# Regrouped PSUM banks, a new TensorE order and earlier loads in a fused attention and mixer kernel

## The chip, the cores and the metric

The kernel runs on one core of a Trainium2 chip. The metric is the device time of one execution in microseconds (us). The kernel before takes 413.0 us (median of three runs, 410.32 to 413.69). Executions are called fast unless the record says otherwise. A profiled execution gives a span a little shorter than its time (414.7 us span for 416.4 us of time).

## The reference

Random-feature attention for 8 batches of 8 heads, 576 positions, head size 64, 128 features; its output x, 8 x 576 x 512, goes through a low-rank mixer and a feed-forward layer of width 2048.

```python
def phi(x):
    proj = np.einsum('bhsd,md->bhsm', x, omega)
    return np.concatenate([np.cos(proj), np.sin(proj)], axis=-1) / np.sqrt(m)
q_p, k_p = phi(q), phi(k)
kv  = np.einsum('bhsm,bhsd->bhmd', k_p, v);  z = np.sum(k_p, axis=2)
num = np.einsum('bhsm,bhmd->bhsd', q_p, kv); den = np.einsum('bhsm,bhm->bhs', q_p, z)
x   = num / den                                  # then (batch, seq, 512)
h   = x.transpose(0, 2, 1) @ U @ V               # rank 32, mixes positions
u   = x + h.transpose(0, 2, 1)
out = u + np.maximum(u @ w_ch1, 0.0) @ w_ch2     # 512 -> 2048 -> 512
```

## The kernel before

The work is cut into 32 groups g (a batch and two heads) and into 43 blocks s, issued in a fixed order on each engine. Block s of the steady part does the angles, sines and cosines of group s, `key_values` and `numerators` of group s - 1, two pairs of hidden tiles (W1) of an earlier batch, and one W2 sum of 16 matmuls in three parts. Every fourth block also mixes a batch (`mix_in`, three `mix_out`). q, k, v come in quads (loads that hold four heads), so quad n serves groups 2n and 2n + 1: GpSimd issues the load that casts them to bf16, and SyncE issues the DMA transposes of k and q. (The first and the fourth quad are transposed on TensorE instead.)

The kernel divides eight banks of PSUM, the buffer that the matmuls write to. The pool with the tag `at` has two slots of two banks each, and almost everything takes its turn there: pk, pt, pq (angles), kv, nd, and hu, hn for mixing. The other four banks hold one pair `h` for hidden tiles and two single banks `ch` for the W2 sums.

```python
    def angles_k(g):
        ...
        pk = psum.tile([P, 2, 512], F32, name="pk", tag="at")
        ...                                   # 8 matmuls
        units(ang[:, 0, 0:1024], pk...)       # VectorE, 1.2 us

    def angles_tail(g, names="kq"):           # the 9th tile of k and of q
        ...
        pt = psum.tile([P, 2, M], F32, name="pt", tag="at")
        ...

    def channel_out(b, t, fs):                # W2
        if 0 in fs:
            ch_of[b] = mm[1].tile([P, C], F32, name="ch_ps", tag="ch")
        for f in fs:
            nc.tensor.matmul(ch_ps, hid[:, f, t * P:(t + 1) * P], W2b[:, f, :], ...)
        if NFT - 1 in fs:
            nc.vector.tensor_tensor(out=o, in0=ch_ps, in1=u[:, t, :], op=ALU.add)
            ...                               # two output DMAs

    def step(s):                              # one block
        loads(s)
        angles_k(s); angles_tail(s); sine(s, 0)
        first(0)                              # hidden pair, tag h
        angles_q(s); sine(s, 1)
        if mb is not None: mix_in(mb)
        second(0)                             # first part of the W2 sum
        key_values(s - 1); cosine(s, 0)
        first(1);          cosine(s, 1)
        if mb is not None: mix_out(mb, 0)
        second(1)
        numerators(s - 1)                     # VectorE: nd -> x
        if mb is not None: mix_out(mb, 1)
        ...                                   # hidden tail, tag ch
        second(2)
        if mb is not None: mix_out(mb, 2)
        ...                                   # W2 tail sum, tag ch
```

(Conditions on s left out.) In the loads, block 5 issues the third W1 part and k, q of the fifth quad, block 6 the fourth v, the fourth W1 part and the first of W2, block 7 the fifth v, W2 and the sixth quad, block 8 the rest of W2.

## Time and profile before

| | before |
|---|---|
| span of the profiled execution | 414.7 us |
| TensorE busy | 364.6 us (88%) |
| blocks 0 to 5, 5 to 11, 11 to 31 (starts) | 44.9, 63.6, 216.1 us |
| from block 31 to the end | 90.1 us |

The start of a block is taken as the start of its first pk matmul. The first lines of the page, kernel before; the columns are busy time, its share, and the number of instructions of each engine:

```profile
span 414.7 us, 8470 instructions
## 1 busy us (share of the span) xinstructions
PE 364.6 (88%) x3662; PEld 187.4 (45%) x3662; DVE 198.4 (48%) x338; ACT 217.7 (52%) x220; POOL 135.4 (33%) x146
```

TensorE (PE) is the bound, and no other engine is above 52%. What matters is where PE idles. The waits of PE from 43 to 112 us, kernel before (us in total, times, longest):

```profile
PE pt L200 <- DMA qT<-qraw: 6.4, 1, 6.4
PE pk L189 <- DVE x L267: 3.6, 3, 1.2
PE pq L210 <- DVE ang L161: 1.9, 2, 1.0
PE pt L198 <- DVE u L301: 1.4, 2, 0.7
PE pt L198 <- DVE x L267: 1.3, 1, 1.3
...
```

One wait is for a DMA: the tail angles of block 8 need the transposed q of the fifth quad. The others wait for VectorE to empty a slot of the shared pair. Two timelines of the kernel before, of SyncE and of PE around block 8 (start us, duration, what, count, and in brackets the idle time before it and who ended it):

```profile
53.42 3.55 SPq L145 DMA_TRANSPOSE kT<-kraw  x1
57.08 8.04 SPq L145 DMA_TRANSPOSE qT<-qraw  x1
```
```profile
70.54 0.21 PE L198 MATMUL pt<-WT,kT 64*128 64x128 bf16 x1 [0.64 <-DVE u L301]
77.16 0.26 PE L200 MATMUL pt<-qT,WT 64*128 64x128 bf16 x1 [6.41 <-DMA qT<-qraw]
77.35 3.60 PE L355 MATMUL h_ps<-uT,W1b 128*128 128x512 bf16 x8
```

The transpose issued at 57.08 us lands at 77.1 us, 20 us later. After the wait the eight hidden matmuls take 3.60 us; they take 1.90 where the clock reads 1.00. The table of stretches shows why: the column after the five engines is the granted clock of PE (the share of the full clock that the chip let it have), then come the busy share of the DMA engines (a value above 1 is read here as full) and GB/s.

```profile
70.00:75.00 5.00, 0.21 (x1) 0.09 (x1) 1.61 (x2) 0.00 (x0) 0.92 (x2) 0.73 1.26 176
75.00:80.00 5.00, 2.84 (x8) 1.00 (x8) 0.42 (x1) 1.16 (x1) 1.13 (x2) 0.50 1.23 204
```

In the steady part such small waits return behind the mixing blocks: pt behind ut in all five from 117 to 330 us, pk behind u in three. PE at the start of block 18, kernel before:

```profile
178.52 0.40 PE L189 MATMUL pk<-WT,kT 64*128 64x128 bf16 x8 [0.72 <-DVE u L301]
179.85 0.21 PE L198 MATMUL pt<-WT,kT 64*128 64x128 bf16 x1 [0.92 <-DVE ut L311]
```

The Trainium skill, "Perfetto Trace Analysis", section "Optimization Strategy", says that consistent bubbles on the engine that should be saturated can mean too little SBUF or PSUM for the next tile. This trace agrees: the slots that pk and pt take were last held by u's and ut's sources.

### The profile page before, as it was taken

How to read it: one execution, taken by the hardware profiler on the slowest of the kernel's cores; microseconds unless marked ns; L12 is line 12 of the kernel's file. 1: busy time of each engine (PE TensorE's matmuls, PEld its weight loads, DVE VectorE, ACT ScalarE, POOL GpSimd, SP SyncE). 2: the span in 40 equal slices, each digit the busy share in tenths (PEclk: the TensorE clock that was granted, in tenths of full speed). 3: DMA queues.
4: the chain of work that ended last, by engine and by line, in shares of the span. 5: the costliest groups of instructions: out<-in, count | busy, mean ns of one | idle time of the engine just before them, and what ended most of it. 6: DMA issues, size and time to landing. Idle time of an engine off the chain costs nothing.

```text
span 414.7 us, 8470 instructions
## 1 busy us (share of the span) xinstructions
PE 364.6 (88%) x3662; PEld 187.4 (45%) x3662; DVE 198.4 (48%) x338; ACT 217.7 (52%) x220; POOL 135.4 (33%) x146
## 2 busy tenths in 40 slices
PE   3367876577999899989999999899999999999995
PEld 2254433233555454434554544445544554445542
DVE  2574675157546645665456555634556535100111
ACT  2882786282487576643664666466665631133300
POOL 7663574243263333520524252524232200000000
PEclk9986998588899999999999999999999999999999
DMA  8987399979673929294738756673913111521133
GB/s 134 177 132 116 63 166 129 195 73 162 95 100 76 164 55 167 43 172 95 120 75 119 114 85 125 97 143 60 157 27 77 27 27 30 109 52 25 27 77 76
DMA packets 73925, 41.07 MB, mean 99 GB/s; under 512 B 52640, under 2 KB 69280, under 8 KB 73888
## 3 DMA queue, kind: packets, MB, share of 16 engines
q1 hardware_dynamic: 55920, 21.96, 32.0%
q0 software_dynamic: 17968, 18.57, 29.8%
q8 instruction: 28, 0.46, 0.4%
q14 instruction: 9, 0.07, 0.1%
HBM read 37.20 MB, written 9.44 MB: 112 GB/s over the span
## 4 chain that ended last, share of the span: by engine, by line
PE 74%; DVE 12%; DMA 8%; issue 2%; ACT 2%; POOL 1%; SPq 0%; DVEq 0%; ACTq 0%; POOLq 0%
PE h_ps L355 26%; PE ch_ps L383 25%; DMA qT<-qraw 7%; PE kv_ps L229 4%; PE nd L251 3%; PE ch_ps L399 3%; DVE x L267 3%; DVE ang L161 3%; PE pq L210 2%; PE ht_ps L371 2%; DVE u L301 2%; DMA kraw<-in_k_dram 2%; DVE nd L262 1%; DVE ut L311 1%; PE nd L257 1%
## 5 line engine op out<-in xcount | busy, mean ns | idle before, releaser
L171 POOL TENSOR_SCALAR ang<-ang 128x1152 int32<-128x1152 int32 x64 | 73.4, 1147 | 186.7 <-ACT ft L170 186.5
L383 PE MATMUL ch_ps<-W2b,hid 128*128 128x512 bf16 x512 | 128.0, 387 | 0.0
L170 ACT ACTIVATE ft<-ang 128x1152 bf16<-128x1152 int16 x64 | 74.1, 1160 | 96.7 <-DVE ang L161 96.0
L355 PE MATMUL h_ps<-uT,W1b 128*128 128x512 bf16 x480 | 116.3, 386 | 0.3 <-ACT hid L359 0.3
L359 ACT ACTIVATE hid<-h_ps 128x1024 bf16<-128x1024 f32 x60 | 61.0, 1016 | 47.2 <-PE h_ps L355 46.4
L177 ACT ACTIVATE ft<-ang 128x1152 bf16<-128x1152 int16 x64 | 73.8, 1155 | 2.4 <-POOL ang L171 2.2
L355 PEld LDWEIGHTS <-W1b 128*128 128x128 bf16 x512 | 46.5, 99 | 60.9 <-issue 9.8
L383 PEld LDWEIGHTS <-hid 128*128 128x128 bf16 x512 | 47.6, 99 | 56.9 <-issue 8.4
L161 DVE TENSOR_SCALAR ang<-pq 128x1024 int32<-128x1024 f32 x32 | 39.2, 1224 | 23.9 <-PE pq L210 23.8
L386 DVE TENSOR_TENSOR o<-ch_ps,u 128x512 f32<-128x512 f32 x32 | 21.9, 685 | 53.4 <-PE ch_ps L383 53.4
L161 DVE TENSOR_SCALAR ang<-pk 128x1024 int32<-128x1024 f32 x32 | 38.9, 1216 | 3.5 <-PE pk L189 3.3
L262 DVE RECIPROCAL nd<-nd 128x10 f32<-128x10 f32 x32 | 7.3, 228 | 63.9 <-PE nd L257 63.8
L229 PEld LDWEIGHTS <-ft 64*128 64x128 bf16 x1152 | 23.8, 101 | 12.0 <-issue 6.3
L301 DVE TENSOR_TENSOR u<-hn,x 128x1024 bf16<-128x1024 f32 x16 | 19.5, 1218 | 12.4 <-PE hn L300 12.3
L251 PEld LDWEIGHTS <-ft 128*128 128x128 bf16 x512 | 21.0, 100 | 9.3 <-ACT ft L170 1.5
L232 DVE CAST kvb<-kv_ps 128x260 bf16<-128x260 f32 x32 | 13.6, 425 | 23.9 <-PE kv_ps L229 23.9
L251 PE MATMUL nd<-kvb,ft 128*128 128x65 bf16 x512 | 22.2, 196 | 1.5 <-DVE kvb L232 1.5
L189 PE MATMUL pk<-WT,kT 64*128 64x128 bf16 x256 | 13.8, 231 | 9.9 <-DVE x L267 3.6
L267 DVE TENSOR_TENSOR x<-nd,rec 128x512 bf16<-128x512 f32 x32 | 21.8, 682 | 0.2
L161 DVE TENSOR_SCALAR ang<-pt 128x256 int32<-128x256 f32 (+1 forms) x33 | 13.4, 405 | 8.5 <-PE pt L200 8.5
L189 PEld LDWEIGHTS <-kT 64*128 64x128 bf16 x256 | 8.5, 99 | 19.7 <-issue 10.5
L210 PE MATMUL pq<-qT,WT 64*128 64x512 bf16 x64 | 13.9, 427 | 3.9 <-DVE ang L161 3.9
(75 smaller groups left out, 282.2 us busy)
## 6 DMA issues: line engine op xcount, KB each, us to landing
out_dram<-o SPq DMA_DIRECT2D x72, 128.0 KB, 2.4
kraw<-in_k_dram POOLq DMA_DIRECT2D x16, 288.0 KB, 4.3
qraw<-in_q_dram POOLq DMA_DIRECT2D x16, 288.0 KB, 6.0
vraw<-in_v_dram POOLq DMA_DIRECT2D x16, 288.0 KB, 6.8
W1b<-in_moe_w_ch_dram POOLq DMA_DIRECT2D x4, 512.0 KB, 5.7
W2b<-in_moe_w_ch_dram POOLq DMA_DIRECT2D x4, 512.0 KB, 16.0
kT<-kraw SPq DMA_TRANSPOSE x14, 4.7
qT<-qraw SPq DMA_TRANSPOSE x14, 4.0
```

The costliest lines, as they stand in the source:

```text
L161: nc.vector.tensor_scalar(out=dst, in0=src, scalar1=TO_UNITS, scalar2=None, op0=ALU.mult)
L170: nc.scalar.activation(out=ft[:, 0, a, :], in_=low, func=ACT.Sin, scale=TO_RAD)
L171: nc.gpsimd.tensor_scalar(out=ang[:, a, :], in0=ang[:, a, :], scalar1=TURN / 4.0, scalar2=1.0, op0=ALU.add, op1=ALU.mult)
L177: nc.scalar.activation(out=ft[:, 1, a, :], in_=low, func=ACT.Sin, scale=TO_RAD)
L189: nc.tensor.matmul(pk[:, e, j * P:(j + 1) * P], kT[r, c, :], WT[r, :])
L229: nc.tensor.matmul(kv_ps[:, hh, o], ft[r, f, 0, c:c + M], vq[n % NV][r, NS * i + s, :], start=(s == 0), stop=(s == NS - 1))
L251: nc.tensor.matmul(nd[:, t // 2, 2 * (t % 2) + hh, :], ft[:, f, 1, c:c + P], kvb[:, hh, f, :], start=(f == 0), stop=(f == 1))
L267: nc.vector.tensor_tensor(out=x[:, :, hp * P:(hp + 1) * P].rearrange("p (a t) (h d) -> p a t h d", a=2, h=2), in0=nd[:, :, 0:4, 0:D], in1= ...
L301: nc.vector.tensor_tensor(out=u[:, 2 * a:2 * a + 2, :], in0=h_ps, in1=x[:, 2 * a:2 * a + 2, :], op=ALU.add)
L355: nc.tensor.matmul(h_f, w1(ct, 2 * i + f), uT[:, :, ct, :], start=(ct == 0), stop=(ct == NCT - 1))
L359: nc.scalar.activation(out=hid[:, 2 * i:2 * i + 2, :], in_=h_ps, func=ACT.Relu)
L383: nc.tensor.matmul(ch_ps, hid[:, f, t * P:(t + 1) * P], W2b[:, f, :], start=(f == 0), stop=(f == NFT - 1))
```

## The change

The intent: whoever takes a slot of the shared pair should find that VectorE has long emptied it. With five users per block (pk, pt, pq, kv, nd) and two slots the slots swap roles from block to block, and pt always takes the slot that nd has just held. The change gives pt a bank of its own (shared with the hidden tail), so an ordinary block has four users; and it moves `mix_in` before `angles_q`, so that a mixing block has eight in a matching order. The bank is taken from the W2 sums, which keep one. In blocks 5 to 8, transposes and `mix_out` go between the two halves of a hidden pair. The fifth k and q, the third W1 part and the fourth v are loaded in the opening; the fifth v moves from block 7 to block 8, the sixth from 8 to 10; the low-rank U, V are issued before the second quad instead of behind it. The first W2 part moves from block 6 to 7, and in the opening the first mixing sums come behind the next block's angles and kv and are copied by ScalarE instead of VectorE. The diff is shortened and its lines put together:

```diff
-        pt = psum.tile([P, 2, M], F32, name="pt", tag="at")
+        pt = (psum.tile([P, 2, M], F32, name="pt", tag="at") if 1 not in mm else
+              mm[1].tile([P, 2, M], F32, name="pt", tag="pt"))
...                                    # hidden tail: tag "ch" -> "pt"; W2 tail sum: "ch" -> "h"
+    def channel_in_apart(b, i, between):          # blocks 5 to 8
+        h_f = mm[1].tile([P, SM], F32, name="h_f", tag="ch")
+        ...                                       # first half, ScalarE empties it
+        between()                                 # transpose_pe(3, "k") or mix_out(0, s - 6)
+        h_f = mm[1].tile([P, SM], F32, name="h_g", tag="h")
+        ...                                       # second half, VectorE empties it
 def step(s):
-        first(0)
+        channel_in(*ins[0])
+        if mb is not None: mix_in(mb)
         angles_q(s); sine(s, 1)
-        if mb is not None: mix_in(mb)
         second(0); key_values(s - 1); cosine(s, 0)
-        first(1); cosine(s, 1)
+        channel_in_tail(...)
         if mb is not None: mix_out(mb, 0)
-        second(1); numerators(s - 1)
+        channel_in(*ins[1]) or channel_in_apart(*ins[1], between)
+        cosine(s, 1); numerators(s - 1); second(1)
         if mb is not None: mix_out(mb, 1)
-        channel_in_tail(...); second(2); mix_out(mb, 2); channel_out_tail(...)
+        channel_out_tail(...); second(2); mix_out(mb, 2)
...
 loads, block 8
+            load(4, "v")
             load_w2(2)
             load_w2(3)
-            load(5, "v")
             widen_v(4)
...
 opening
     load(0, "v")
+    load_low_rank()
     load(1, "kqv")
-    load_low_rank()
...
     widen_v(2)
+    load_w1(2)
+    load(3, "v")
+    load(4, "kq")
+    transpose_dma(4)
...                                    # first mixing sums issued after angles_k(4), key_values(3)
-    mm[1] = ctx.enter_context(tc.tile_pool(name="psum1", bufs=2, ...))
+    mm[1] = ctx.enter_context(tc.tile_pool(name="psum1", bufs=1, ...))
```

More of the change, by code (lines that the diff above doesn't have):

```diff
@@ L340, with hidden, channel_in @@
     hid_of, ch_of = {}, {}
-    def channel_in(b, i, tag):
-        uT = u_of["T", b]
+    def hidden(b, f, h_f):
+        for ct in range(NCT):
+            nc.tensor.matmul(h_f, w1(ct, f), u_of["T", b][:, :, ct, :], start=(ct == 0), stop=(ct == NCT - 1))
+    def channel_in(b, i):
         if i == 0:
             hid_of[b] = hidp.tile([P, NFT, SM], BF16, name="hid")
-        hid = hid_of[b]
-        if tag == "h":
-            h_ps = mm[1].tile([P, 2, SM], F32, name="h_ps", tag="h", bufs=1)
+        h_ps = mm[1].tile([P, 2, SM], F32, name="h_ps", tag="h")
         for f in range(2):
-            if tag == "ch":
-                h_f = mm[1].tile([P, SM], F32, name="h_f", tag="ch")
-            else:
-                h_f = h_ps[:, f, :]
-            for ct in range(NCT):
-                nc.tensor.matmul(h_f, w1(ct, 2 * i + f), uT[:, :, ct, :], start=(ct == 0), stop=(ct == NCT - 1))
-            if tag == "ch":
-                nc.scalar.activation(out=hid[:, 2 * i + f, :], in_=h_f, func=ACT.Relu)
-        if tag == "h":
-            nc.scalar.activation(out=hid[:, 2 * i:2 * i + 2, :], in_=h_ps, func=ACT.Relu)
-        if i == NFT // 2 - 1:
-            u_of.pop(("T", b))
+            hidden(b, 2 * i + f, h_ps[:, f, :])
+        nc.scalar.activation(out=hid_of[b][:, 2 * i:2 * i + 2, :], in_=h_ps, func=ACT.Relu)
+    def channel_in_apart(b, i, between):
+        h_f = mm[1].tile([P, SM], F32, name="h_f", tag="ch")
+        hidden(b, 2 * i, h_f)
+        nc.scalar.activation(out=hid_of[b][:, 2 * i, :], in_=h_f, func=ACT.Relu)
+        between()
+        h_f = mm[1].tile([P, SM], F32, name="h_g", tag="h")
+        hidden(b, 2 * i + 1, h_f)
+        nc.vector.tensor_scalar(out=hid_of[b][:, 2 * i + 1, :], in0=h_f, scalar1=0.0, scalar2=None, op0=ALU.max)
     def channel_in_tail(bp, i):
@@ L367, in channel_in_tail @@
         hid = hid_of["tail", bp]
-        h_ps = mm[1].tile([P, 4, P], F32, name="ht_ps", tag="ch")
+        h_ps = mm[1].tile([P, 4, P], F32, name="ht_ps", tag="pt")
         for f in range(4):
@@ L396, in channel_out_tail @@
         hid = hid_of.pop(("tail", bp))
-        ch_ps = mm[1].tile([P, C], F32, name="ch_ps", tag="ch")
+        ch_ps = mm[1].tile([P, C], F32, name="ct_ps", tag="h")
         for f in range(NFT):
@@ L426, in step @@
         mb = (s - 5) // 4 if s % 4 == 1 and s > 5 and s // 4 <= B else None
-        def first(i):
-            if i < len(ins):
-                b, j = ins[i]
-                channel_in(b, j, "ch" if i == 1 and not outs else "h")
         def second(i):
@@ L435, in second, with between @@
                 channel_out(*outs[i])
+        def between():
+            if s == 5:
+                transpose_pe(3, "k", nc.vector.tensor_copy, psum, "at")
+            elif s <= 8:
+                mix_out(0, s - 6)
         loads(s)
@@ L443, in step @@
             second(0)
-        first(0)
+        if ins:
+            channel_in(*ins[0])
+        if mb is not None:
+            mix_in(mb)
         if s < NG:
@@ L447, in step @@
             sine(s, 1)
-        if mb is not None:
-            mix_in(mb)
         if s != 11:
@@ L455, in step @@
             cosine(s, 0)
-        first(1)
+        if ins and ins[0][0] % 2 == 1:
+            channel_in_tail(ins[0][0] // 2, ins[0][1] // 2)
+        if mb is not None:
+            mix_out(mb, 0)
+        if ins and outs:
+            channel_in(*ins[1])
+        elif ins:
+            channel_in_apart(*ins[1], between)
         if s < NG:
             cosine(s, 1)
-        if mb is not None:
-            mix_out(mb, 0)
-        second(1)
+        if s == 5:
+            transpose_pe(3, "q", nc.vector.tensor_copy, psum, "at")
         if s <= NG:
             numerators(s - 1)
+        second(1)
         if mb is not None:
             mix_out(mb, 1)
-        if ins and ins[0][0] % 2 == 1:
-            channel_in_tail(ins[0][0] // 2, ins[0][1] // 2)
+        if outs and outs[0][0] % 2 == 1 and outs[0][1] == NT - 1:
+            channel_out_tail(outs[0][0] // 2)
         second(2)
@@ L470, in step @@
             mix_out(mb, 2)
-        if s in (6, 7, 8):
-            mix_out(0, s - 6)
-        if outs and outs[0][0] % 2 == 1 and outs[0][1] == NT - 1:
-            channel_out_tail(outs[0][0] // 2)
     def loads(s):
         n = s // 2 + 1
-        if s == 5:
-            load_w1(2)
-            load(4, "kq")
-            for name in "kq":
-                transpose_pe(3, name, nc.vector.tensor_copy, psum, "at")
-            transpose_dma(4)
-        elif s == 6:
-            load(3, "v")
+        if s == 6:
+            widen_v(3)
             load_w1(3)
+        elif s == 7:
             load_w2(0)
-            widen_v(3)
-        elif s == 7:
-            load(4, "v")
-            load_w2(1)
             load(5, "kq")
             transpose_dma(5)
+            load_w2(1)
         elif s == 8:
+            load(4, "v")
             load_w2(2)
             load_w2(3)
+            widen_v(4)
+        elif s == 10:
             load(5, "v")
-            widen_v(4)
+            load(6, "kqv")
+            transpose_dma(6)
+            widen_v(5)
         elif s % 2 == 0 and n < NG // 2:
@@ L565 @@
     numerators(2)
-    hu_out = mix_first_in(range(0, 3))
-    hu_out(nc.vector.tensor_copy)
     angles_k(4)
@@ L570 @@
     key_values(3)
+    mix_first_in(range(0, 3))(nc.scalar.copy)
+    sine(4, 0)
+    numerators(3)
     t_a = psum.tile([P, 2, SM], F32, name="tx", tag="at")
-    for i in range(2):
-        mix_first_T(i, t_a[:, i, :])()
-        mix_first_out(i, t_a[:, i, :], nc.scalar.copy)
     t_b = psum.tile([P, 2, SM], F32, name="tx", tag="at")
-    mix_first_T(2, t_b[:, 0, :])()
-    mix_first_out(2, t_b[:, 0, :], nc.scalar.copy)
-    numerators(3)
-    hu_out = mix_first_in(range(3, 4))
-    close = mix_first_T(3, t_b[:, 1, :])
-    hu_out(nc.vector.tensor_copy)
+    tx = [t_a[:, 0, :], t_a[:, 1, :], t_b[:, 0, :], t_b[:, 1, :]]
+    for i in range(3):
+        mix_first_T(i, tx[i])()
+        mix_first_out(i, tx[i], nc.scalar.copy)
+    close = mix_first_T(3, tx[3])
+    mix_first_in(range(3, 4))(nc.vector.tensor_copy)
     close()
-    sine(4, 0)
-    mix_first_out(3, t_b[:, 1, :], nc.vector.tensor_copy, range(0, 2))
-    mix_first_out(3, t_b[:, 1, :], nc.scalar.copy, range(2, 4))
+    mix_first_out(3, tx[3], nc.vector.tensor_copy, range(0, 2))
+    mix_first_out(3, tx[3], nc.scalar.copy, range(2, 4))
     angles_q(4)
@@ L590 @@
     opening.close()
-    mm[1] = ctx.enter_context(tc.tile_pool(name="psum1", bufs=2, space=bass.MemoryType.PSUM))
+    mm[1] = ctx.enter_context(tc.tile_pool(name="psum1", bufs=1, space=bass.MemoryType.PSUM))
     for s in range(5, NG + 11):
```

## The prediction

> **What bounds the kernel now.** TensorE. The page shows PE busy 364.6 of 414.7 us (88%); the chain of waits is 74% PE. By stretches, from 120 to 340 us PE has 18 to 20 us of work in each 20 us. The loss is early: 38 of the 50 idle us fall before 120 us. PE's waits, by stretch:
> - 0 to 43 us (start, first mixing): about 20 us; 3.0 for the first mixing sum behind x, 1.5 for kvb, 2.0 for pq behind the angles.
> - 43 to 112 us (blocks 5 to 10): 17.4 us. One of 6.4 us, at 70.5 us: block 8's tail angles wait for the fifth q's transpose, which took 20.0 us to land, while the table of stretches shows DMA full from 51 to 88 us (and at zero from 40 to 45 us). The rest are 0.3 to 1.3 us each: pk, pq, pt behind x, ang, u, ut, which hold the two slots of the shared PSUM pair.
> - 112 to 330 us: 7.4 us of that kind (ut 3.6, u 2.2, x 1.1).
>
> In blocks 7 to 10 the idling also lowers the granted clock (0.50 to 0.75 in several 5 us stretches). A hidden pair's eight matmuls took 3.60 us after the 6.4 us wait, 1.90 otherwise. This agrees with the Trainium skill, "TensorE: Matmul & The Clock Gate", Part 1 (after an idle window half the clock, until a busy window has passed). From the stretched groups I estimate 7 us.
>
> **What the change does.** No matmul is removed; the floor stays.
> 1. Fifth k, q are loaded and transposed some 10 us earlier, where DMA is idle; the third W1 part and the fourth v too. The 6.4 us wait and its cold clock (2.4 us) should go: -8.5.
> 2. pt has its own bank, the order gives each slot one more block before reuse, and transposes and mix_out move between the halves of the hidden work. Of 10 us of small waits in blocks 5 to 10 plus 4 us of cold clock I expect over half back: -8. From 112 us on, 5 of 7.4: -5.
> 3. First mixing: sums come after the next block's angles and kv: -3.
>
> Costs:
> - W2 sums have one bank, not two. In the last blocks nothing stands between one sum and the next, so PE waits for the eviction (0.69 us plus signalling) three times: +2.5.
> - The low-rank loads now precede the second quad (three issues, 1.9 us on POOL), whose transpose is on the early chain: +1.
> - Block 8 loads and widens the fifth v at once, behind W2 parts; POOL waits for it and holds the cosine: +2.
>
> Sum: -24.5 + 5.5 = -19; I take 17, for waits that reappear elsewhere.
>
> **Prediction: 396 us, range 388 to 405.** Faster by over 2%: 0.88, within 2%: 0.11, slower: 0.01.
>
> **What would show it right or wrong.** PE's waits: none of several us for qT near block 8; pk, pt, pq behind u, ut, x under 4 us in total after the opening; no clock below 0.9 between 60 and 110 us. Block 5's start to block 11's shrinks from 65 to about 50 us. PE busy falls by several us by the clock alone. At the end ch_ps waits for o three times, near 0.9 us each.
>
> **What would make it wrong.** The fifth or sixth quad's transposes land late (the sixth's slot may come free only late); v of block 8 or W2 stalls; ScalarE, with more in a row, holds the single pair of hidden banks; the opening slows by more than 1 us.

## The result, and the profile after

The changed kernel takes 400.06 us (median of four runs, 398.77 to 401.19) beside 412.38 for the kernel before. The ratio is 0.9705, 95% interval 0.965 to 0.9759. A ratio here is the mean time of one kernel's fast runs over that of the other's of the same rounds, so not quite the ratio of the medians.

The page, changed kernel:

```profile
span 398.9 us, 8471 instructions
## 1 busy us (share of the span) xinstructions
PE 356.6 (89%) x3662; PEld 185.1 (46%) x3662; DVE 200.7 (50%) x341; ACT 213.8 (54%) x217; POOL 135.2 (34%) x146
```

The same number of matmuls is busy for 8.0 us less, which I put down to the clock (the mean granted clock is 0.991 instead of 0.958). The rest of the difference is idle time. By block starts, in us, with the version E4 of the experiments beside it:

| stretch | before | changed | difference | E4 |
|---|---|---|---|---|
| start to block 3 | 23.7 | 28.2 | +4.5 | 24.1 |
| blocks 3 to 5 | 21.2 | 17.2 | -4.0 | 17.2 |
| blocks 5 to 11 | 63.6 | 50.6 | -13.0 | 47.3 |
| block 11 | 8.9 | 9.1 | +0.3 | 8.9 |
| blocks 12 to 31 | 207.2 | 199.6 | -7.6 | 199.6 |
| from block 31 to the end | 90.1 | 94.2 | +4.1 | 90.4 |
| span | 414.7 | 398.9 | -15.8 | 387.5 |

The profiled executions differ by 15.8 us, the medians by 12.3: the profiled one of before (416.4 us of time) was the slow end of its runs. The opening varies: in six profiles whose opening code is that of the changed kernel (it, its repeat, E2, E3, E7, E8) block 5 begins between 43.6 and 47.8 us, and blocks 3 to 5 take 16.4 to 19.5 us. Blocks 12 to 31 repeat to 0.01 us.

What went as meant. Block 8 and block 18 in the changed kernel, the counterparts of the lines above (L189 is pk, L199 and L201 are pt, L345 is the hidden tiles):

```profile
67.88 0.22 PE L201 MATMUL pt<-qT,WT 64*128 64x128 bf16 x1
68.02 1.90 PE L345 MATMUL h_ps<-uT,W1b 128*128 128x512 bf16 x8
...
163.48 0.40 PE L189 MATMUL pk<-WT,kT 64*128 64x128 bf16 x8
163.71 0.22 PE L199 MATMUL pt<-WT,kT 64*128 64x128 bf16 x1
163.77 0.22 PE L201 MATMUL pt<-qT,WT 64*128 64x128 bf16 x1
```

No brackets: PE waits for nothing there.

What was lost. Three waits stand out in the PE timelines, two of them new. The second quad's transposed q in the opening was waited for 2.42 us before and 7.01 us after; the first W2 sum in block 9 and each W2 sum of the last batch wait only in the changed kernel. Kernel before, where the last batch's matmuls stand in one row:

```profile
20.89 0.26 PE L200 MATMUL pt<-qT,WT 64*128 64x128 bf16 x1 [2.42 <-DMA qT<-qraw]
...
391.60 15.06 PE L383 MATMUL ch_ps<-W2b,hid 128*128 128x512 bf16 x69
```

Changed kernel:

```profile
25.39 0.26 PE L201 MATMUL pt<-qT,WT 64*128 64x128 bf16 x1 [7.01 <-DMA qT<-qraw]
...
80.19 2.72 PE L384 MATMUL ch_ps<-W2b,hid 128*128 128x512 bf16 x6 [2.61 <-ACT hid L358]
...
373.90 3.61 PE L384 MATMUL ch_ps<-W2b,hid 128*128 128x512 bf16 x16 [0.78 <-DVE o L387]
378.29 3.61 PE L384 MATMUL ch_ps<-W2b,hid 128*128 128x512 bf16 x16 [0.78 <-DVE o L387]
```

The second of them can be followed backwards. GpSimd and ScalarE, changed kernel:

```profile
68.17 0.73 POOL L137 DMA_DIRECT2D vraw<-in_v_dram  x1
68.89 1.51 POOL L118 DMA_DIRECT2D W2b<-in_moe_w_ch_dram  x2
...
76.19 1.15 POOL L140 COPY vq_103<-vraw 128x1152 bf16<-128x1152 bf16 x1 [5.79 <-DMA vraw<-in_v_dram]
77.31 2.27 POOL L171 TENSOR_SCALAR ang<-ang 128x1152 int32<-128x1152 int32 x2
78.48 1.16 ACT L177 ACTIVATE ft<-ang 128x1152 bf16<-128x1152 int16 x1 [4.65 <-POOL ang L171]
79.56 0.58 ACT L358 ACTIVATE hid<-h_f 128x512 bf16<-128x512 f32 x1
```

GpSimd waits 5.8 us for the v that it asked for in the same block, its addition for the cosine stands behind that wait, ScalarE waits for the addition, and the eviction of a hidden half stands behind the cosine. A copy that is off the critical path thus stops PE, through two engines that here did their work in the order in which it was issued. The clock follows: 0.51 from 80 to 85 us.

### The profile page after: what moved, and what is told of

It is laid out like the page before. It is cut to its first block, busy times and chain, and to the rows that moved or that the text cites. A ratio compares the mean times of both kernels' runs of the same rounds, so it can differ in the third digit from the quotient of the medians.

```text
span 398.9 us, 8471 instructions
## 1 busy us (share of the span) xinstructions
PE 356.6 (89%) x3662; PEld 185.1 (46%) x3662; DVE 200.7 (50%) x341; ACT 213.8 (54%) x217; POOL 135.2 (34%) x146
## 4 chain that ended last, share of the span: by engine, by line
PE 73%; DMA 9%; DVE 8%; ACT 4%; issue 2%; POOL 2%; ACTq 0%; DVEq 0%; POOLq 0%
PE ch_ps L384 26%; PE h_ps L345 24%; PE ht_ps L372 4%; PE ct_ps L400 4%; PE kv_ps L230 4%; PE nd L252 3%; DVE ang L161 3%; DMA qT<-qraw 3%; DMA uT<-u 2%; ACT ft L170 2%; DMA qraw<-in_q_dram 2%; DMA vraw<-in_v_dram 2%; PE pk L189 2%; PE pq L211 2%; PE hn L301 1%
## 5 line engine op out<-in xcount | busy, mean ns | idle before, releaser
L384 PE MATMUL ch_ps<-W2b,hid 128*128 128x512 bf16 x512 | 124.0, 382 | 6.1 <-DVE o L387 3.5
L345 PE MATMUL h_ps<-uT,W1b 128*128 128x512 bf16 x480 | 113.7, 380 | 1.2 <-ACT hid L353 0.9
L384 PEld LDWEIGHTS <-hid 128*128 128x128 bf16 x512 | 46.8, 98 | 61.8 <-issue 13.5
L345 PEld LDWEIGHTS <-W1b 128*128 128x128 bf16 x512 | 46.7, 98 | 56.0 <-issue 5.0
L230 PEld LDWEIGHTS <-ft 64*128 64x128 bf16 x1152 | 23.0, 99 | 12.2 <-issue 8.2
L252 PE MATMUL nd<-kvb,ft 128*128 128x65 bf16 x512 | 22.7, 198 | 2.1 <-DVE kvb L233 2.1
L189 PE MATMUL pk<-WT,kT 64*128 64x128 bf16 x256 | 13.8, 232 | 4.9 <-DMA kT<-kraw 2.3
L372 PE MATMUL ht_ps<-utT,W1b 128*128 128x128 bf16 x256 | 17.0, 219 | 0.0
```

The lines of the kernel that those rows point to most:

```text
L230: nc.tensor.matmul(kv_ps[:, hh, o], ft[r, f, 0, c:c + M], vq[n % NV][r, NS * i + s, :], start=(s == 0), stop=(s == NS - 1))
L252: nc.tensor.matmul(nd[:, t // 2, 2 * (t % 2) + hh, :], ft[:, f, 1, c:c + P], kvb[:, hh, f, :], start=(f == 0), stop=(f == 1))
L345: nc.tensor.matmul(h_f, w1(ct, f), u_of["T", b][:, :, ct, :], start=(ct == 0), stop=(ct == NCT - 1))
L372: nc.tensor.matmul(h_ps[:, f, :], w1(ct, 4 * i + f), utT[:, ct, :], start=(ct == 0), stop=(ct == NCT - 1))
```

## The experiments

Twelve kernels ran, in three jobs, all with five rounds against the kernel before on the same chip. The changed kernel itself ran only in the first job (with E1 to E3); E4, E5, E7, E8 ran in the second and E6, E9 to E11 in the third, each on another chip. Differences to the changed kernel are the difference of the two ratios times 412 us. Each ratio has an interval of about 0.5% to either side, so such a difference is uncertain by about 3 us. The profiles tell stretches apart much more finely.

### The changed kernel again

> The changed kernel again, as the yardstick of this job: 0.970 of the kernel before, span near 398.9 us, the wait of the tail angles for the second quad's q transpose 7.0 us, W2 sums behind the last hidden eviction 2.6 us, W2 sums behind the output adds 3.1 us at the end.

Measured: 0.9734 (0.9683 to 0.9785), median 400.64 us. All ratios below are set against this one. Its opening was luckier: qT waited 6.0 us, block 5 began at 43.6 us.

### E1: low-rank loads behind the second quad again

```diff
     load(0, "v")
-    load_low_rank()
     load(1, "kqv")
+    load_low_rank()
```

> The changed kernel with the low-rank loads issued after the second quad again. Theory A (moving them delayed the second quad's q transpose, issued 2.3 us later, into the third quad's loads): the wait for qT falls from 7.0 to near 2.4 us, block 3 starts near 23.7 instead of 28.2 us, and most of it stays to the end: 2.5 to 4.5 us faster than the changed kernel. Theory B (the opening is bound by ScalarE and VectorE chains and DMA later on, so the delay is absorbed by block 5): block 5's start and the total move by under 1 us.

Measured: 0.9613 (0.9567 to 0.9659), median 395.75 us: 5.0 us faster than the changed kernel. The wait of PE for qT fell to 2.4 us and block 3 began at 24.4 us:

```profile
21.56 0.26 PE L201 MATMUL pt<-qT,WT 64*128 64x128 bf16 x1 [2.44 <-DMA qT<-qraw]
```

Theory A held in the time. The profiled execution alone would have supported B: it was the slowest of the six (398.4 us; the others 395.0 to 396.6), because its clock was low from 29 to 39 us, so block 5 began only 0.5 us before that of the changed kernel's second profile.

### E2: the fifth v loaded in block 6

```diff
         if s == 6:
             widen_v(3)
+            load(4, "v")
             load_w1(3)
...
         elif s == 8:
-            load(4, "v")
             load_w2(2)
```

> The changed kernel with the fifth v loaded in block 6 instead of block 8, where it is widened. Theory A (the stall of block 9, 2.6 us behind the hidden eviction and 1.1 us behind x, with its low clock, comes from GpSimd waiting 5.8 us for this v, which holds the cosine and with it ScalarE's eviction): GpSimd's wait under 1 us, block 9 takes 10.5 to 11.5 instead of 14.2 us, total 3 to 4.5 us faster. Theory B (W2's parts or the sixth quad's transposes would hold block 9 or 10 next, since DMA is full then): block 9 or 10 waits for these instead, total within 1 us.

Measured: 0.9686 (0.9637 to 0.9736), median 399.13 us: 2.0 us faster, which by itself is not clear of zero. The profile is clear. GpSimd does not wait for that v any more, the W2 sum of block 9 follows at once, and the clock column reads 1.00 in every stretch from 70 to 90 us:

```profile
69.97 1.18 POOL L140 COPY vq<-vraw 128x1152 bf16<-128x1152 bf16 x1
```
```profile
77.48 0.39 PE L211 MATMUL pq<-qT,WT 64*128 64x512 bf16 x2 [0.41 <-DVE ang L161]
77.81 1.47 PE L384 MATMUL ch_ps<-W2b,hid 128*128 128x512 bf16 x5
```

Block 9 took 9.5 instead of 14.2 us (in E4 and E11, which have the same edit, it took 11.0 and 9.5). The 1.1 us wait behind x stayed: that part of theory A was wrong. Of the 4.8 us, about 1 went into a later wait for the transposed u of block 11 (1.2 us instead of 0.3), so B is true in small.

### E3: two banks for the last W2 sums

```diff
-            ch_of[b] = mm[1].tile([P, C], F32, name="ch_ps", tag="ch")
+            ch_of[b] = mm[1].tile([P, C], F32, name="ch_ps",
+                                  tag="pt" if b == B - 1 and t % 2 == 0 else "ch")
```

> The changed kernel with the last batch's W2 sums alternating between the ch bank and the pt bank, which is free there. Theory A (one bank for the W2 sums costs four waits of 0.78 us in the last blocks): the four waits go, total 3.1 us faster. Theory B (the end is set by something else, such as the output's path): under 1 us.

Measured: 0.9623 (0.958 to 0.9667), median 396.12 us: 4.6 us faster. The four waits are gone; the last batch's matmuls stand in one row:

```profile
370.89 14.84 PE L384 MATMUL ch_ps<-W2b,hid 128*128 128x512 bf16 x67
```

From block 31 to the end it takes 90.4 instead of 94.2 us, 3.8 less. That is more than the waits of 0.78 us: in the changed kernel sums start 4.39 us apart (378.29 - 373.90), without the wait 3.45 us apart (the spacing of the output adds in the profile of before), so each change of sum costs 0.94 us.

### E4: all three

> The changed kernel with all three mends: low-rank loads after the second quad, fifth v loaded in block 6, last W2 sums in two banks. If the three costs are separate: 4.9 + 2 + 4.5 us off the changed kernel, near 389 us, 0.945 of the kernel before. If they share one slack (the opening's gain was seen to be absorbed by block 5 in one profile), near 393 us.

Measured: 0.9491 (0.9453 to 0.9529), median 389.74 us, 10.0 us faster than the changed kernel. E1 to E3 add up to 11.6, so within the uncertainty the three costs are separate, and this version beats both kernels. Its stretches are in the table above: the opening and the end are those of before, and the rest is that of the changed kernel or better.

### E5: in the kernel before, the fifth k and q loaded early

```diff
     widen_v(2)
+    load(4, "kq")
     nc.gpsimd.tensor_copy(Vb, ...)
...
         if s == 5:
             load_w1(2)
-            load(4, "kq")
```

> The kernel before with one thing changed: the fifth k and q are loaded in the opening, behind the third v's widening; their transposes stay in block 5, the orders and banks stay. Theory A (block 8's stall and its cold clock are this quad's lateness alone): the wait of 6.4 us for qT goes, block 8 takes about 9 instead of 17 us, total 7 to 9 us faster than before, 0.98. Theory B (DMA is full from 51 to 88 us, so the stall only moves to another transfer, W2 or v): total within 3 us of before.

Measured: 0.9885 (0.9843 to 0.9927), 4.7 us faster than before; two of the six runs are marked slow (412.1 and 415.6 us, clock 0.974) and are left out. In the profile the wait for qT is gone, block 8 takes 9.7 instead of 17.1 us, and blocks 5 to 11 take 51.8 instead of 63.6 us, for block 10 had its full clock too (7.9 instead of 10.6 us). The small waits all stay:

```profile
70.13 0.40 PE L189 MATMUL pk<-WT,kT 64*128 64x128 bf16 x8 [1.43 <-DVE x L267]
71.16 0.26 PE L198 MATMUL pt<-WT,kT 64*128 64x128 bf16 x1 [0.64 <-DVE u L301]
71.47 3.42 PE L355 MATMUL h_ps<-uT,W1b 128*128 128x512 bf16 x8
```

Most of this group's low clock therefore does not come from the long wait: the hidden matmuls take 3.42 us without it and 3.60 with it. Of the 7.4 us that block 8 lost, 6.4 are the wait and about 1 the rest, clock above all. So the wait's cause is shown, its "cold clock" only in part. The gain in time was about half of the expected 7 to 9 us, and where the executions lost it is not known; in the profiled one the opening was 2.1 us longer, all of it by block 3, before the moved loads are issued.

### E6: in the changed kernel, the fifth k and q loaded late

```diff
-    load(4, "kq")
-    transpose_dma(4)                 # opening
...
+        if s == 5:
+            load(4, "kq")
+            transpose_dma(4)
```

> The changed kernel with the fifth k and q loaded and transposed at the start of block 5 again; the third W1 part and the fourth v stay early. Theory A (this quad's early load is worth what its lateness cost before): the wait for qT in block 8 returns, 5 us or more with its cold clock, blocks 5 to 11 take 56 us or more instead of 50.6, total 5 to 8 us slower than the changed kernel. Theory B (W1's and v's early loads already emptied the queue enough): no wait over 1 us in block 8, total within 2 us.

Measured: the five fast runs give 0.9732 (0.9684 to 0.978), 0.1 us from the changed kernel. By the time, theory B held: once the third W1 part and the fourth v are out of the way, this quad may come as late as before. With E5 this says that either is enough: to ask for this quad early while the others stay (E5), or, as far as the time shows, to ask for the others early while this quad stays (E6). The kernel before with only the third W1 part and the fourth v early was not run. The profiled execution was the remaining one, and took 1956.78 us: its matmuls were three to six times slower, while the other engines were busy about as long as ever.

```profile
PE 1935.2 (99%) x3662; PEld 655.9 (34%) x3662; DVE 206.6 (11%) x341; ACT 220.7 (11%) x217; POOL 135.2 (7%) x146
```

It says nothing about the change, so block 8 of this kernel in a fast run was not seen.

### E7: the banks of before, with the new order

```diff
+        pt = psum.tile([P, 2, M], F32, name="pt", tag="at")
-                    tag="pt" / tag="h"                 # hidden tail, W2 tail sum
+                    tag="ch", bufs=2                   # these, the W2 sums and h_f
```

> The changed kernel with the banks of before and the new order: pt in the shared pair, two single banks for W2 sums, tail sums and tail hidden. Theory A (pt's own bank is what lets the order work; with pt in the pair each block takes five slots and the next user comes one block later): waits of pk, pq, pt behind DVE return, 5 to 8 us from block 11 to 31, but the 3.1 us at the end go: 3 to 5 us slower than the changed kernel. Theory B (the order alone does it): blocks 11 to 31 within 1 us, total 3 us faster than the changed kernel.

Measured: 0.9942 (0.9904 to 0.9979), median 408.52 us: 8.6 us slower than the changed kernel. Blocks 12 to 31 take 204.3 instead of 199.6 us, the end 4.0 us less. The waits of PE from 117 to 330 us:

```profile
PE pt L198 <- DVE ut L311: 3.5, 5, 0.9
...
PE pk L189 <- DVE u L301: 0.7, 1, 0.7
PE pt L198 <- DVE x L267: 0.6, 2, 0.4
```

pt waits again, as theory A says; pk behind u stays cured by the order alone (0.7 us; 2.2 before). The loss is larger than expected: in the profile block 11 took 3.2 us more (it waits 2.6 us for u's transpose, instead of 0.3), blocks 5 to 11 1.3 us more, and the opening, whose code is the same, 2.4 us more by its clock. The wait in block 11 need not come from the banks: E8, whose code is that of the changed kernel up to block 11, waits 2.2 us there.

### E8: the new banks, with the order of before from block 12 on

```diff
     for s in range(5, NG + 11):
-        step(s)
+        (step_old if s >= 12 else step)(s)      # step_old: the order of before, the new banks
```

> The changed kernel with the new banks, and from block 12 on the order of before. Theory A (banks and order are needed together): waits of 0.3 to 1 us behind u, ut, x return in the blocks that mix; blocks 12 to 31 take 4 to 6 us more than the 199.6 us of the changed kernel. Theory B (the banks alone do it): blocks 12 to 31 within 1 us of it.

Measured: 0.9851 (0.9817 to 0.9885), median 405.38 us: 4.8 us slower. Blocks 12 to 31 take 203.3 us, block 11 12.6 instead of 9.1. The waits of PE from 117 to 330 us:

```profile
PE pk L189 <- DVE u L302: 2.2, 3, 0.7
PE ch_ps L384 <- issue: 2.1, 13, 0.2
PE pt L199 <- ACT hidt L374: 0.7, 2, 0.4
PE h_ps L345 <- ACT hid L353: 0.7, 2, 0.3
PE h_ps L345 <- DVE o L402: 0.7, 2, 0.3
```

pt behind ut is cured by its bank, pk behind u is back, and the shared new banks bring small waits of their own. ("issue" is time in which PE waited for nothing that the profile shows.) From 207.2 us, the banks alone save 4.0 (E8), the order alone 2.9 (E7), both 7.6 us. The two act nearly independently; the theory "needed together" was too strong, and so was "one of them does it".

### E9: the first mixing in the order of before

The opening's part from `key_values(3)` to `mix_first_out(3)` is put back as it was, on top of the changed kernel.

> The changed kernel with the first mixing in the order of before. Theory A (the new order is worth the 3 us of the prediction): blocks 3 to 5 take 3 to 4 us more than in the changed kernel (17.2 us), total 3 us slower. Theory B (the second quad's late transpose makes the opening DMA-bound, so the order there is absorbed): total within 1.5 us.

Measured: 0.9802 (0.976 to 0.9843), median 402.70 us, 2.8 us slower, at the edge of what the times can tell; beside E6, which ran in the same job and has the new order, it is 2.9 us (means of the fast runs, 403.0 and 400.1). Blocks 3 to 5 take 20.2 instead of 17.2 us, and PE again waits 1.5 and 1.4 us before the two groups of mixing sums. But this 3.0 us is not the order alone. With the new order blocks 3 to 5 took 19.5 us in E3 and in E7. There three of the four large matmuls of the first mixing took 1.06 us, in E9 two, in the changed kernel none (0.59 each). Against E3 and E7, E9 is only 0.7 us longer. The times favour theory A; how much of the 3 us is order and how much clock stays open.

### E10: the third quad's loads later

```diff
-    load(2, "kq")
-    transpose_dma(2)                 # behind angles_tail(1)
...
     widen_v(1)
+    load(2, "kq")
+    transpose_dma(2)
```

> The changed kernel, low-rank loads first as it has them, but the third quad's k and q are issued behind the second v's widening (near 20 us instead of 14.7). Theory A (the second q's transpose took 10.4 us because the third quad's loads ran beside it): it lands in about 5 us, near 20 us, block 3 starts near 23 instead of 28.2 us, the total falls by 2 us or more, unless the third quad, 5 us later, stalls block 4. Theory B (the transpose is slow because of the low-rank loads themselves): it still takes 8 us or more.

Measured: 0.9793 (0.9751 to 0.9835), median 402.75 us, 2.4 us slower, not clear of zero. The mechanism of theory A is plain: the second q's transpose, issued at 15.29 us, has landed when pt starts at 18.97 us, 3.7 us later. In the changed kernel the chain of waits shows 10.4 us for it:

```profile
14.94 10.41 DMA qT<-qraw
```

The low-rank loads are where the change put them in both kernels, so they are not what slows the transpose; the third quad's loads beside it are. But the gain is given back at block 4, which then waits for the third quad itself (PE, E10):

```profile
18.97 0.26 PE L201 MATMUL pt<-qT,WT 64*128 64x128 bf16 x1 [0.23 <-DMA qT<-qraw]
...
34.99 0.61 PE L189 MATMUL pk<-WT,kT 64*128 64x128 bf16 x8 [6.15 <-DMA kT<-kraw]
...
39.31 0.26 PE L201 MATMUL pt<-qT,WT 64*128 64x128 bf16 x1 [3.61 <-DMA qT<-qraw]
```

### E11: E4, with the third quad's loads later

> The kernel with the three mends, and the third quad's loads later as well. If the second q's transpose still shares DMA with these loads there (it lands near 21.5 us): block 3 starts 1 to 2 us earlier, total 388 to 389 us. If the third quad becomes late instead: 390 to 392 us.

Measured: 0.9679 (0.9636 to 0.9722), median 398.17 us: 7.7 us slower than E4, far outside what was expected. Block 3 began 1.4 us earlier (22.7 us), block 5 8.4 us later (49.7 us), behind the same two waits. E4 stays the best.

## Why the prediction was right

The time, 400.1 us, lies in the range of 388 to 405, above the 396 named, and the class was right. The waits and the costs were the ones named, with one exception under item 1. That the sum came so near is in part luck: by the profiles the gains were larger than the 24.5 us said (about 29, though against the slow end of the kernel before), and the costs were about double the 5.5 us said (11.6 us in time, E1 to E3). By its steps:

- **Item 1, "the 6.4 us wait and its cold clock should go: -8.5".** The wait went, and with it blocks 8 and 10 fell by 10.1 us in the profile of E5; in time E5 gained 4.7 us. The cold clock was misplaced: block 8 won about 1 us by it, not 2.4, as the hidden matmuls stayed slow without the wait (3.42 us). The item names the early fifth quad and the early W1 part and v together. The quad alone is enough in the kernel before (E5), and it is not needed once the other two come early (E6: 0.1 us). The second half is shown for the time only; E6 has no usable profile.
- **Item 2, small waits: -8 in blocks 5 to 10 and -5 from 112 us on.** Blocks 5 to 11 lost 13.0 us, against -14.5 that items 1 and 2 and the cost of v give together; what the transposes and mix_out between the halves of the hidden work bring by themselves was not tested. Blocks 12 to 31 lost 7.6 us, more than the 5: of 7.1 us of waits for u, ut and x 1.0 is left. Banks and order bring about half each (E7, E8).
- **Item 3, first mixing: -3.** E9 gives 2.8 us in time, at the edge of the noise; its 3.0 us in the profile shrink to 0.7 beside executions with a like clock, so the size is not shown.
- **Cost of one W2 bank: +2.5.** The end took 4.1 us more. There are four such changes of sum, not three, and each costs 0.94 us (E3).
- **Cost of the low-rank loads: +1.** This is the term that was most mis-sized: block 3 began 4.5 us later, and undoing it gained 5.0 us (E1). The estimate took the 1.9 us of issue; the issue moved the transpose by 2.3 us into the third quad's loads, and there it took 10.4 us instead of the 8.2 us of before, or the 3.7 us that it takes without these loads (E10).
- **Cost of the fifth v: +2.** In the profile 4.8 us in block 9 (E2; 3.2 in E4), by the chain that was named; in time 2.0 us, not clear of zero.

Of its signs, "no clock below 0.9 between 60 and 110 us" was wrong (0.51 from 80 to 85 us, through that stall), and "no wait of several us for qT" was right near block 8 but not in the opening. PE busy fell by 8.0 us, blocks 5 to 11 from 63.6 to 50.6 us (65 to 50 was said), and after the opening pk, pt and pq wait for u, ut and x only 1.5 us in all. With the opening and the end sized right (+3.5 and +1.6 us more), the sum would have been about 401 us.

## What to carry to other kernels

Count the users of a rotating buffer per iteration, and see which user always comes right behind the slow one. Here an even count for two slots and a bank of its own for one small user removed waits without touching any work. The bank that is given up must be looked at where nothing stands between two of its users. Transposes of one size took 3.7 to 20.0 us here, by what was in flight beside it, so before a load is moved, look what it will then run beside: 2 us of issue order cost 5 us here, and putting off the competitor cost more than it gave. An engine that is far from busy (GpSimd, 34%) can still stop the bottleneck when it waits for a transfer in front of work that others need.

## What the Trainium skill lacked or had wrong

- "DMA: Bandwidth & Descriptors", section "Issuing engines are not separate DMA queues", says that DMAs of all issuing engines run on the same 16 engines and interleave. The traces agree, but no page gives the size for a transpose next to ordinary loads: one of 128 partitions x 1152 bf16 elements landed in 3.7 us without the third quad's loads (E10), in 10.4 us beside these two loads of 288 KB, and in 20.0 us in the stretch where DMA was full. The same page's "Rules for kernel authors" says of a transpose next to ordinary DMAs that it "needs nothing"; that is about correctness, and the results were correct in every run of the experiments. It says nothing of the time.
- "TensorE: Matmul & The Clock Gate", Part 1, warns that clock events in a trace are unreliable. Here the granted clock reads 1.00 from 25 to 35 us in the changed kernel, while 16 nd matmuls take 1.06 us there and 0.67 us later: up to the first event the record shows no low clock. Durations of a known group are the safer sign. Which clock the opening gets differs between executions of the same code (the matmuls of the first mixing take 0.59 or 1.06 us).
- The same page tells of a clock stuck at a quarter for 50 us. One execution of E6 ran slow from start to end: ten W2 matmuls took 13.14 us instead of 2.16, a factor of 6.1. Its trace holds no clock event, so the recorded clock of 1.0 is no measurement. No page has a factor of six; its cause is open.
- No page gives the cost of a PSUM bank with one buffer between accumulation groups: here 0.94 us per change, of which 0.69 us is the eviction of 128 x 512 fp32.
